# Clustered attention and a routed expert layer on one core: GpSimd's scatters and gathers given fixed places among its low parts, and the first expert's w1 split by way of PSUM

## The chip, the cores and the metric

The kernel runs on one core of one Trainium2 chip. The metric is the device time of one execution in microseconds; lower is better. The engines are named as the profile names them: PE (TensorE, matrix multiplies, with PEld for its weight loads), DVE (VectorE), ACT (ScalarE), POOL (GpSimd) and SP (SyncE, which here only issues DMAs). Each engine takes its own instructions strictly in order. The on-chip memory is SBUF, the accumulators of PE are eight banks of PSUM, and DRAM is the memory outside.

## The reference, cut to what is computed

Attention within clusters (batch 4, 8 heads, 768 positions, head size 64, 16 clusters), whose output rows go through a two-level router to one of 16 experts:

```python
q_assign = argmax(q_n @ c_n.T); k_assign = argmax(k_n @ c_n.T)   # nearest of 16 centroids
mask = q_assign[:, None] == k_assign[None, :]
scores = where(mask, q @ k.T / 8, -1e9)
attn = softmax(scores); x = attn @ v                              # rows: 4*768 tokens of 512
g_idx = argmax(x @ w_group)                                       # 4 groups
e_idx = argmax(x @ w_expert[g_idx])                               # 4 experts in each
h = maximum(x @ w1[g, e], 0.0)                                    # 512 -> 1024
out = g_w * e_w * (h @ w2[g, e])                                  # 1024 -> 512, gates are softmax values
```

Every product is made in 16-bit parts: a float32 number is written as a high part and a low part (what the high part leaves), and the products of the parts are added in PSUM.

## The kernel before, in words

**Attention.** The loop goes over 32 heads (4 batches of 8) and, in each head, over 9 units `u`; a unit is 512 columns of the score matrix. For unit number g, PE makes the fine scores (`fine`, tile `psf`, two banks), ACT takes the exponential into `p` (line 347), and the low part `pl` is made by one subtraction, on GpSimd for all units but some of the last two heads (line 349). That subtraction is called a low part below. Five units later (`LAG = 5`) PE multiplies high and low part with V (`av`, tile `pso`, lines 366 and 367). Eighteen units ahead PE makes the coarse scores of a later head (`coarse`, tile `psc`, two banks), of which DVE takes the row maxima (line 305). The last coarse unit is number 287, so PE makes none from unit 270 on. Beside the units run the splits of q, k and v, the cluster masks and the end of each head (lines 380 to 387), at places given by a table of unit numbers. Work that needs a bank of the small pool `psm` (two banks) takes turns: a generator yields `PSM` and is called when its turn comes, one turn in each unit.

**Router.** After the last head of a batch b, `logits` and `decide` work out each token's expert and its row in a table in DRAM. `decide` then scatters 6 x 128 rows of token number and gate into that table, one indirect DMA of GpSimd for each of 6 columns (line 668), and yields 5 units before each (4 for batch 2). The Tile scheduler, which puts the instructions into each engine's order, is free to move such a DMA ahead in GpSimd's order, since it depends on no low part.

**First expert.** After batch 2 has been decided, `first` picks the expert with most tokens so far, loads its w1 (four chunks of 128 x 1024 float32, tile `st`, four buffers) and splits each chunk: ACT writes the high part `wh` (line 758), and DVE makes the low part `wl` by one instruction with both tensors in SBUF (line 761). Then `first` reads that expert's rows of the table (`tabA`, three DMAs on SP's queue, which wait until all scatters so far have landed), turns them into `idA` (DVE, line 816), gathers 288 token rows with three indirect DMAs of GpSimd (line 889, into the buffers `qx`, `kx` and `vx`), and transposes them on PE (line 899) near the end of attention. `FIRST` is the number of units that it lets pass after each step.

**Experts.** After attention come the first expert, then the 15 others and an overflow block, with weights streamed through `st`; the change does not touch that part.

`issue_after(x)` makes the scheduler put what is made under it behind instruction x; where both are on one engine, this only sets the order there.

Of the kernel before, what the change touches and what calls it, by code (L numbers as in the profile page):

```python
# [13 lines left out]
F32 = mybir.dt.float32  # L14
I32 = mybir.dt.int32
AF = mybir.ActivationFunctionType
ALU = mybir.AluOpType
AX = mybir.AxisListType
ET = mybir.EngineType
# [3 lines left out]
P = 128  # L23
SQ = 16.0
XS = 128.0
WS = 32.0
# [1 line left out]
WRS = 16.0  # L28
PSHIFT = 55.4375
PSM = "psm"  # L30
FIRST = 4

def attention(ctx, tc, qT, kT, vr, cen, R, DEN, cfg):
    nc = tc.nc
# [11 lines left out]
    NH = B * H  # L46
# [288 lines left out]
    def fine(h, u):  # L335
        assert ("max", h) in ready
        pf = ps_f.tile([P, 512], F32, name="psf")
        off = 0
        for (c, q0, q1) in fsegs(u):
            o = pf[:, off:off + q1 - q0]  # L340
            ks = slice(c * P, (c + 1) * P)
            nc.tensor.matmul(out=o, lhsT=KA[h % 8][0:82, ks], rhs=QA[h % 8][0:82, q0:q1], start=True, stop=False)  # L342
            nc.tensor.matmul(out=o, lhsT=KBs[h][:, ks], rhs=QBs[h][:, q0:q1], start=False, stop=True)  # L343
            off += q1 - q0
        p32 = pp.tile([P, 512], F32, name="p32")
        pl = pp.tile([P, 512], F16, name="pl")
        cfg["exp"] = nc.scalar.activation(out=p32, in_=pf, func=AF.Exp, scale=QK / (SQ * SQ))  # L347
        ph = p32.bitcast(BF16)[:, 1::2]
        (nc.vector if u in (EARLY if h < 2 else DVE_LO[h % 8] if h < NH - 2 else DVE_END) else nc.gpsimd).tensor_tensor(out=pl, in0=p32, in1=ph, op=ALU.subtract)  # L349
        Ph[h, u], Pl[h, u] = ph, pl  # L350

    def av(h, u):
# [168 lines left out]
class Router:  # L521
    def __init__(self, ctx, tc, wr, xbuf, table, N, E, BS, cfg):
        nc = self.nc = tc.nc
        self.tc, self.xbuf, self.table, self.N, self.E, self.BS = tc, xbuf, table, N, E, BS
        const = ctx.enter_context(tc.tile_pool(name="rconst", bufs=1))
        self.sm = ctx.enter_context(tc.tile_pool(name="rsm", bufs=1))
        self.ident = cfg["ident"]
        KD = self.KD = wr.shape[1]
        self.const, self.wr = const, wr

# [81 lines left out]
    def decide(self, b, early=None, then=None):  # L612
# [52 lines left out]
        for c in range(T):  # L665
            for _ in range(1 if early else 4 if then else 5):
                yield
            d = self.last["p"] = nc.gpsimd.indirect_dma_start(
                out=self.table, out_offset=bass.IndirectOffsetOnAxis(ap=di[:, c:c + 1], axis=0),
                in_=self.pay[:, t0 + c], in_offset=None)  # L670
            if self.apart:

                self.alone(d, "sent", self.sent)
# [18 lines left out]
class Experts:  # L692
# [61 lines left out]
    def split_chunk(self, st, hi, lo, i, q, eng):  # L754
# [5 lines left out]
            nc.gpsimd.tensor_scalar(out=h, in0=st, scalar1=WS, scalar2=0.0, op0=ALU.mult, op1=ALU.add)  # L760
        nc.vector.scalar_tensor_tensor(out=l, in0=st, scalar=WS, in1=h, op0=ALU.mult, op1=ALU.subtract)

    def wtiles(self, pool, i, n=""):
        w = (self.w1, self.w2)[i]
        sh = [P, w.shape[1] // P, w.shape[2]]
        return [pool.tile(sh, F16, name=f"w{a}{i}{n}") for a in "hl"]
# [4 lines left out]
    def first(self):  # L771

        nc, R, E = self.nc, self.R, self.R.E
        t = self.small("ft", [P, E])
        m = self.small("fm", [P, 1])
        nc.vector.tensor_tensor(out=self.cntA, in0=R.cb, in1=R.ebase, op=ALU.subtract)
        nc.vector.scalar_tensor_tensor(out=t, in0=self.cntA, scalar=float(2 * E), in1=self.io, op0=ALU.mult, op1=ALU.subtract)
        nc.vector.tensor_reduce(out=m, in_=t, axis=AX.X, op=ALU.max)
        nc.vector.tensor_scalar(out=self.oh0, in0=t, scalar1=m, scalar2=None, op0=ALU.is_equal)
        nc.vector.tensor_tensor(out=t, in0=self.oh0, in1=self.io, op=ALU.mult)  # L780
        nc.vector.tensor_reduce(out=self.f0f, in_=t, axis=AX.X, op=ALU.add)
        nc.vector.tensor_copy(out=self.f0i, in_=self.f0f)

        nc.vector.tensor_scalar(out=t, in0=R.cb, scalar1=-1.0, scalar2=float(E * R.BS), op0=ALU.mult, op1=ALU.add)
        nc.vector.tensor_tensor(out=t, in0=t, in1=self.oh0, op=ALU.mult)
        nc.vector.tensor_tensor(out=R.cb, in0=R.cb, in1=t, op=ALU.add)
        yield
        self.f0 = self.load_reg(self.f0i[0:1, 0:1], E - 1)
        self.WA = self.wtiles(self.wa, 0)
        after = lambda: self.tc.issue_after(self.cfg["exp"].ins) if "exp" in self.cfg else ExitStack()  # L790
        chunks = []
        for q in range(4 + 2):
            if q < 4:
                chunks.append(self.load_chunk(0, self.f0, q))
            if q >= 2:
                with after():
                    self.split_chunk(chunks[q - 2], *self.WA, 0, q - 2, 0)
            for _ in range(FIRST):
                yield

        CA, KD = self.CA, R.KD
        nt = -(-CA // P)
        sz = [min(P, CA - t * P) for t in range(nt)]
        tab = self.small("tabA", [P, nt, 2])
        tv = R.table.rearrange("(e s) w -> e s w", s=R.BS)[bass.ds(self.f0, 1)].rearrange("e s w -> (e s) w")
        while R.done < R.B - 2:
            yield
        for t, n in enumerate(sz):
            R.reads(nc.sync.dma_start(out=tab[0:n, t], in_=tv[t * P:t * P + n]))
        self.w2A = [self.load_chunk(1, self.f0, 0)]  # L810
        for _ in range(FIRST):
            yield
        ids = self.small("idA", [P, nt], I32)
        g = self.small("gA", [P, nt])
        for t, n in enumerate(sz):
            nc.vector.tensor_copy(out=ids[0:n, t:t + 1], in_=tab[0:n, t, 0:1])
            nc.vector.tensor_scalar(out=g[0:n, t:t + 1], in0=tab[0:n, t, 1:2], scalar1=1.0 / (XS * WS * WS), scalar2=None, op0=ALU.mult)
        self.colsA = [g[0:n, t:t + 1] for t, n in enumerate(sz)], [ids[0:n, t:t + 1] for t, n in enumerate(sz)]

        rows = R.N - R.N // R.B  # L820
        xgs = []
        for t, n in enumerate(sz):
            self.w2A.append(self.load_chunk(1, self.f0, t + 1))
            xf = self.cfg["ld"].tile([P, KD * P * 3 // 2], F32, name=("qx", "kx", "vx")[t])[:, 0:self.D]
            nc.vector.memset(xf, 0.0)
            xgs.append(xf.bitcast(F16).rearrange("p (a d) -> p a d", a=2))
            if rows:
                self.gather(ids[0:n, t:t + 1], n, xgs[t], rows)
            for _ in range(4):
                yield  # L830
        self.xTA = self.wa.tile([P, 2, KD, CA], F16, name="xTA")
        for t, n in enumerate(sz):
            yield PSM, 2, 2
            with after():
                self.transposed(self.xTA, xgs[t], t, n, R.psm.tile([P, 512], F32, name="psm"))
            yield

# [548 lines left out]
```

## Time and profile before

| What | Value |
|---|---|
| Time, median of 3 runs | 810.94 us (809.08 to 813.51) |
| Profiled execution | 810.6 us, with a span of 808.9 us in the trace |
| Attention in the span | to about 440 us |
| PE busy | 738.6 us (91%) |
| DVE, POOL, ACT busy | 621.1, 497.0, 460.0 us |
| Mean granted clock of PE | 0.963 |

The span is what the trace covers, the time is that of the whole execution, 1.7 us more. PE is the engine with the most work; it is in order, so each of its pauses in attention is a unit that comes later. The share of busy time says little of a single place: what matters is where PE pauses, what released it, and at what clock it went on.

### The profile page before, as it was taken

Reading aid. Unit: us, or ns where it says so; the run is one execution under the profiler, and the core shown is the slowest. Engines: PE = TensorE matmul, PEld = TensorE weight load, DVE = VectorE, ACT = ScalarE, POOL = GpSimd, SP = SyncE. Lnnn points to the kernel's source line nnn. Section 1 sums busy time; section 2 is a strip of 40 time slices with the busy share of each in tenths; the row PEclk is TensorE's granted clock in tenths of the full one; section 3 lists DMA queues with packets and bytes.
Section 4 is the critical chain, followed back from the end, with each engine's and each line's share of the span. In section 5 each row is a group of like instructions: output and inputs, shape, how many; then the busy total and the mean of one; then the engine's idle time right before and its main releaser. Section 6 shows DMA issues by size and latency. Waiting matters only on the chain. (4 is left out here: it accounts for less than half of the span.)

```text
span 808.9 us, 26554 instructions
## 1 busy us (share of the span) xinstructions
PE 738.6 (91%) x11034; PEld 627.1 (78%) x11034; DVE 621.1 (77%) x1193; ACT 460.0 (57%) x893; POOL 497.0 (61%) x497
## 2 busy tenths in 40 slices
PE   5899999989999899997699868999999999999992
PEld 3677788768887688875588655788779999999991
DVE  6998879878798788988865645767589988887840
ACT  4567868658686587765366445435544454555431
POOL 9487787697877878769663424525556544654330
PEclk6899999999999999999799989999999999999996
DMA  8856435235343352223210287866687678888700
GB/s 235 210 155 154 127 100 163 77 90 146 103 138 101 90 144 67 68 74 106 92 41 4 80 296 254 260 215 216 220 262 246 225 246 261 263 274 270 234 30 18
DMA packets 80616, 128.54 MB, mean 159 GB/s; under 512 B 9011, under 2 KB 47411, under 8 KB 80488
## 3 DMA queue, kind: packets, MB, share of 16 engines
q1 hardware_dynamic: 74636, 113.12, 46.8%
q0 software_dynamic: 5696, 13.61, 4.7%
q8 instruction: 88, 1.44, 0.8%
q14 instruction: 40, 0.33, 0.1%
q10 hardware_dynamic: 156, 0.03, 0.0%
HBM read 93.47 MB, written 14.11 MB: 133 GB/s over the span
## 5 line engine op out<-in xcount | busy, mean ns | idle before, releaser
L349 POOL TENSOR_TENSOR pl<-p 128x512 f16<-128x512 f32 x278 | 288.6, 1054 | 98.2 <-ACT p L347 93.8
L305 DVE TENSOR_REDUCE mpart<-psc 128x1 f32<-128x512 f32 (+1 forms) x282 | 190.3, 684 | 47.1 <-PE psc L302 46.6
L347 ACT ACTIVATE p<-psf 128x512 f32<-128x512 f32 x288 | 169.3, 595 | 80.3 <-PE psf L343 72.2
L366 PE MATMUL pso<-V,pl 128*128 128x65 f16 x1152 | 164.0, 195 | 5.5 <-POOL pl L349 5.3
L366 PE MATMUL pso<-V,p 128*128 128x65 f16 x1152 | 164.6, 195 | 0.8 <-issue 0.6
L367 PE MATMUL pso<-V,p 128*128 128x64 f16 x1152 | 163.7, 193 | 0.0
L367 PE MATMUL pso<-V,pl 128*128 128x64 f16 x1152 | 163.7, 192 | 0.0
L342 PE MATMUL psf<-A 82*128 82x384 f16 (+2 forms) x576 | 144.9, 277 | 2.3 <-DMA A<-mr 0.9
L343 PE MATMUL psf<-B 128*128 128x384 f16 (+2 forms) x576 | 145.1, 277 | 0.0
L367 PEld LDWEIGHTS <-p 128*128 128x128 bf16 x1152 | 113.6, 99 | 22.2 <-issue 1.5
L366 PEld LDWEIGHTS <-p 128*128 128x128 bf16 x1152 | 113.2, 98 | 16.8 <-issue 8.9
L302 PE MATMUL psc<-A 80*128 80x512 f16 (+1 forms) x376 | 109.7, 333 | 15.7 <-DVE mpart L305 14.4
L366 PEld LDWEIGHTS <-pl 128*128 128x128 f16 x1152 | 112.3, 97 | 6.5 <-POOL pl L349 5.9
L367 PEld LDWEIGHTS <-pl 128*128 128x128 f16 x1152 | 113.8, 99 | 0.6 <-issue 0.3
L930 DVE SCALAR_TENSOR_TENSOR hl<-psh,hh 128x160 f16<-128x160 f32 (+14 forms) x136 | 50.1, 370 | 56.4 <-ACT hh L929 47.2
L929 ACT ACTIVATE hh<-psh 128x160 f16<-128x160 f32 (+14 forms) x136 | 46.1, 346 | 64.8 <-PE psh L927 63.7
L927 PE MATMUL psh<-xT,wh0a 128*128 128x288 f16 (+7 forms) x512 | 75.6, 256 | 0.9 <-issue 0.5
L988 POOL DMA_INDIRECT out_dram<-y,ri x32 | 38.9, 1215 | 60.3 <-ACT y L987 55.2
L927 PE MATMUL psh<-xT,wh0b 128*128 128x272 f16 (+6 forms) x448 | 65.2, 254 | 1.6 <-ACT xT L901 1.2
L343 PEld LDWEIGHTS <-B 128*128 128x128 f16 x576 | 56.9, 99 | 11.2 <-issue 3.0
L342 PEld LDWEIGHTS <-A 82*128 82x128 f16 x576 | 55.9, 98 | 12.3 <-DMA A<-mr 1.0
L927 PE MATMUL psh<-xT,wl0a 128*128 128x288 f16 (+7 forms) x256 | 64.4, 256 | 1.0 <-issue 1.0
(297 smaller groups left out, 1747.5 us busy)
## 6 DMA issues: line engine op xcount, KB each, us to landing
st<-w SPq DMA_DIRECT2D x128, 512.0 KB
B<-parts SPq DMA_DIRECT2D x64, 192.0 KB
kx<-kT SPq DMA_DIRECT2D x16, 384.0 KB
qx<-qT SPq DMA_DIRECT2D x16, 384.0 KB
vx<-vr SPq DMA_DIRECT2D x16, 384.0 KB
A<-parts SPq DMA_DIRECT2D x32, 192.0 KB
xbuf<-xs SPq DMA_DIRECT2D x4, 1536.0 KB
A<-mk SPq DMA_DIRECT2D x56, 24.0 KB
```

What stands on the lines that cost most here:

```text
L302: last["mm"] = nc.tensor.matmul(out=pc[:, off:off + k1 - k0], lhsT=QA[h % 8][0:80, c * P:(c + 1) * P], rhs=KA[h % 8][0:80, k0:k1], start=T ...
L305: nc.vector.tensor_reduce(out=(mp[:, 0, 0:1], mp[:, :, 1], mp[:, 1, 0:1])[i], in_=pc.rearrange("p (a x) -> p a x", a=n), axis=AX.X, op=ALU ...
L342: nc.tensor.matmul(out=o, lhsT=KA[h % 8][0:82, ks], rhs=QA[h % 8][0:82, q0:q1], start=True, stop=False)
L343: nc.tensor.matmul(out=o, lhsT=KBs[h][:, ks], rhs=QBs[h][:, q0:q1], start=False, stop=True)
L347: cfg["exp"] = nc.scalar.activation(out=p32, in_=pf, func=AF.Exp, scale=QK / (SQ * SQ))
L349: (nc.vector if u in (EARLY if h < 2 else DVE_LO[h % 8] if h < NH - 2 else DVE_END) else nc.gpsimd).tensor_tensor(out=pl, in0=p32, in1=ph, ...
L366: nc.tensor.matmul(out=O[:, col:col + 65], lhsT=p[:, bs], rhs=vh, start=c == 0 and q == 0 and i == 0, stop=False, skip_group_check=True)
L367: nc.tensor.matmul(out=O[:, col:col + 64], lhsT=p[:, bs], rhs=vl, start=False, stop=c == NCH - 1 and i == 1, skip_group_check=True)
L927: self.mm = nc.tensor.matmul(out=ph[:, 0:M], lhsT=w[:, k, fs], rhs=xT[:, a, k], start=i == 0, stop=i == 3 * KD - 1)
L929: nc.scalar.activation(out=hh[:, f], in_=ph[:, 0:M], func=AF.Relu)
L930: self.ev = nc.vector.scalar_tensor_tensor(out=hl[:, f], in0=ph[:, 0:M], scalar=0.0, in1=hh[:, f], op0=ALU.max, op1=ALU.subtract)
L988: d = nc.gpsimd.indirect_dma_start(out=self.out, out_offset=bass.IndirectOffsetOnAxis(ap=idc, axis=0), in_=y[0:n], in_offset=None, bounds_ ...
```

## The change

Three things are changed. The table scatters of batches 0 to 2 and the three gathers of the first expert are each placed behind the latest low part that was given to GpSimd (`cfg["lo"]`). The w1 split of the first expert becomes `split_beside`: the high part as before, and then for each half of a chunk ACT writes the scaled float32 values to a bank of `psm` and DVE subtracts the high part from there; each half takes a turn in the small pool. `FIRST` goes from 4 units to 2 (3 behind the reading of the table).

```diff
-FIRST = 4
+FIRST = 2
...
-        (nc.vector if u in (EARLY if h < 2 else DVE_LO[h % 8] if h < NH - 2 else DVE_END) else nc.gpsimd).tensor_tensor(out=pl, in0=p32, in1=ph, op=ALU.subtract)
+        lo = (nc.vector if u in (EARLY if h < 2 else DVE_LO[h % 8] if h < NH - 2 else DVE_END) else nc.gpsimd).tensor_tensor(out=pl, in0=p32, in1=ph, op=ALU.subtract)
+        if lo.ins.engine == ET.Pool:
+            cfg["lo"] = lo
...
-            d = self.last["p"] = nc.gpsimd.indirect_dma_start(
-                out=self.table, out_offset=bass.IndirectOffsetOnAxis(ap=di[:, c:c + 1], axis=0),
-                in_=self.pay[:, t0 + c], in_offset=None)
+            with self.tc.issue_after(self.cfg["lo"].ins) if self.apart and not early and "lo" in self.cfg else ExitStack():
+                d = self.last["p"] = nc.gpsimd.indirect_dma_start(
+                    out=self.table, out_offset=bass.IndirectOffsetOnAxis(ap=di[:, c:c + 1], axis=0),
+                    in_=self.pay[:, t0 + c], in_offset=None)
...
+    def split_beside(self, st, hi, lo, i, q):
+
+        nc = self.nc
+        h, l = (w[:, *self.part(i, q)] for w in (hi, lo))
+        with self.after():
+            nc.scalar.activation(out=h, in_=st, func=AF.Copy, scale=WS)
+        n = st.shape[1] // 2
+        for j in range(2):
+            yield PSM, 1, 1
+            rows = slice(j * n, j * n + n)
+            t = self.R.psm.tile([P, 512], F32, name="psm").rearrange("p (a b) -> p a b", a=n)
+            with self.after():
+                nc.scalar.activation(out=t, in_=st[:, rows], func=AF.Copy, scale=WS)
+            nc.vector.tensor_tensor(out=l[:, rows], in0=t, in1=h[:, rows], op=ALU.subtract)
...
             if q >= 2:
-                with after():
-                    self.split_chunk(chunks[q - 2], *self.WA, 0, q - 2, 0)
+                yield from self.split_beside(chunks[q - 2], *self.WA, 0, q - 2)
             for _ in range(FIRST):
                 yield
...
         self.w2A = [self.load_chunk(1, self.f0, 0)]
-        for _ in range(FIRST):
+        for _ in range(FIRST + 1):
             yield
...
             if rows:
-                self.gather(ids[0:n, t:t + 1], n, xgs[t], rows)
+                with self.tc.issue_after(self.cfg["lo"].ins) if "lo" in self.cfg else ExitStack():
+                    self.gather(ids[0:n, t:t + 1], n, xgs[t], rows)
```

In the rows below, which list an engine's instructions in order, L is the line of the code, then come the operation and out<-in; a number behind a name tells buffers apart. Line numbers of the changed kernel are up to 21 higher, and 20 lines stand between L816 before and L836 after.

First, GpSimd behind batch 0, where the scatters (`table<-pay,rdi`) go in among the low parts. Before:

```order
L349 TENSOR_TENSOR pl<-p_4053 128x512
L668 DMA table<-pay,rdi 54400x2
L349 TENSOR_TENSOR pl<-p_4082 128x512
L668 DMA table<-pay,rdi 54400x2 x2
L349 TENSOR_TENSOR pl<-p_4116 128x512
L668 DMA table<-pay,rdi 54400x2
L349 TENSOR_TENSOR pl<-p_4145 128x512
L668 DMA table<-pay,rdi 54400x2 x2
L349 TENSOR_TENSOR pl<-p_4173 128x512
```

The same place after:

```order
L349 TENSOR_TENSOR pl<-p_4145 128x512
L349 TENSOR_TENSOR pl<-p_4173 128x512
L672 DMA table<-pay,rdi 54400x2
L349 TENSOR_TENSOR pl<-p_4206 128x512
L349 TENSOR_TENSOR pl<-p_4246 128x512
L349 TENSOR_TENSOR pl<-p_4277 128x512
L349 TENSOR_TENSOR pl<-p_4310 128x512
L349 TENSOR_TENSOR pl<-p_4348 128x512
L672 DMA table<-pay,rdi 54400x2
```

Six scatters among four low parts become one scatter behind every fifth low part; behind batch 1 it is the same, and behind batch 2 there are four low parts between two scatters.

Second, GpSimd at the sixth scatter of batch 2 and the gathers of the first expert (`qx<-xbuf,idA` and so on). Before, the first gather stood nine low parts behind that scatter (`p_9647` is the p of unit 242):

```order
L668 DMA table<-pay,rdi 54400x2
L349 TENSOR_TENSOR pl<-p_9647 128x512
L349 TENSOR_TENSOR pl<-p_9676 128x512
L349 TENSOR_TENSOR pl<-p_9710 128x512
L349 TENSOR_TENSOR pl<-p_9739 128x512
L349 TENSOR_TENSOR pl<-p_9769 128x512
L349 TENSOR_TENSOR pl<-p_9809 128x512
L349 TENSOR_TENSOR pl<-p_9850 128x512
L349 TENSOR_TENSOR pl<-p_9889 128x512
L349 TENSOR_TENSOR pl<-p_9925 128x512
L889 DMA qx<-xbuf,idA 128x1024
```

After (`p_10329` is the p of unit 262, and `p_10470` that of unit 266):

```order
L349 TENSOR_TENSOR pl<-p_10329 128x512
L672 DMA table<-pay,rdi 54400x2
L349 TENSOR_TENSOR pl<-p_10359 128x512
L349 TENSOR_TENSOR pl<-p_10395 128x512
L349 TENSOR_TENSOR pl<-p_10433 128x512
L349 TENSOR_TENSOR pl<-p_10470 128x512
L910 DMA qx<-xbuf,idA 128x1024
L349 TENSOR_TENSOR pl<-p_10524 128x512
L349 TENSOR_TENSOR pl<-p_10560 128x512
L349 TENSOR_TENSOR pl<-p_10591 128x512
L910 DMA kx<-xbuf,idA 128x1024
```

The sixth scatter has moved 21 units back, and the first gather stands four low parts behind it.

Third, DVE around the split of w1 and the reading of the table (`mpart<-psc` are the row maxima of the coarse scores). Before:

```order
L761 SCALAR_TENSOR_TENSOR wl_9582<-st,wh_9581 128x2x512
L387 TENSOR_TENSOR xs<-pso,xs 128x6x64
L305 TENSOR_REDUCE mpart_200<-psc 128x1 x2
L600 COPY lg<-psm 128x60
L305 TENSOR_REDUCE mpart_200<-psc 128x2
L816 CAST idA<-tabA 128x1
```

After, at the end of the split, the last half and what follows it:

```order
L783 TENSOR_TENSOR wl_9582<-psm,wh_9581 128x512
L305 TENSOR_REDUCE mpart_199<-psc 128x2
L305 TENSOR_REDUCE mpart_199<-psc 128x1 x2
L305 TENSOR_REDUCE mpart_199<-psc 128x2
L382 TENSOR_SCALAR DEN<-pso 128x6
L384 RECIPROCAL rec<-DEN 128x6
L387 TENSOR_TENSOR pso<-pso,rec 128x6x64
L305 TENSOR_REDUCE mpart_199<-psc 128x1
L389 TENSOR_TENSOR xs<-pso,xs 128x6x64
L836 CAST idA<-tabA 128x1
```

The four instructions of 1024 columns have become eight of 512, all ahead of `idA`, and `idA` now stands between the sixth and the seventh coarse unit of the last head. On SP's queue the three loads of `tabA` have moved behind two of the loads `A<-mr` (row maxima) and all four loads of the first expert's w2 follow them.

More of the change, by code (lines that the diff above doesn't have):

```diff
@@ L526, in __init__ @@
         self.sm = ctx.enter_context(tc.tile_pool(name="rsm", bufs=1))
-        self.ident = cfg["ident"]
+        self.ident, self.cfg = cfg["ident"], cfg
         KD = self.KD = wr.shape[1]
@@ L761, in split_chunk, with after @@
         nc.vector.scalar_tensor_tensor(out=l, in0=st, scalar=WS, in1=h, op0=ALU.mult, op1=ALU.subtract)
+    def after(self):
+        return self.tc.issue_after(self.cfg["exp"].ins) if "exp" in self.cfg else ExitStack()
+    def split_beside(self, st, hi, lo, i, q):
[11 more added lines that the diff above has]
+            nc.vector.tensor_tensor(out=l[:, rows], in0=t, in1=h[:, rows], op=ALU.subtract)
     def wtiles(self, pool, i, n=""):
@@ L789, in first @@
         self.WA = self.wtiles(self.wa, 0)
-        after = lambda: self.tc.issue_after(self.cfg["exp"].ins) if "exp" in self.cfg else ExitStack()
         chunks = []
@@ L833, in first @@
             yield PSM, 2, 2
-            with after():
+            with self.after():
                 self.transposed(self.xTA, xgs[t], t, n, R.psm.tile([P, 512], F32, name="psm"))
```

## The prediction

> **What bounds the kernel now.** I read the page first: PE's busy slices and its clock.
>
> ```profile
> PE   5899999989999899997699868999999999999992
> PEclk6899999999999999999799989999999999999996
> ```
>
> PE is nearly full from the second slice on. It dips in slices 18 to 19 (364 to 404 us) and a little in 8 and 13, inside attention; the dips at 23 lie behind it, where nothing is moved. So I took PE's busy time by windows around those places (start:end, length, then PE, PEld, DVE, ACT, POOL busy with counts, clock, DMA share, GB/s).
>
> ```profile
> 168.00:175.10 7.10, 3.96 (x67) 3.03 (x65) 4.74 (x9) 3.06 (x6) 6.38 (x8) 0.99 0.57 141
> 175.10:178.30 3.20, 3.18 (x36) 2.37 (x37) 0.62 (x1) 1.24 (x3) 3.20 (x4) 0.50 0.00 0
> 270.00:277.40 7.40, 4.51 (x78) 3.44 (x77) 4.85 (x9) 3.25 (x7) 6.68 (x8) 0.99 0.55 137
> 277.40:280.90 3.50, 3.50 (x60) 2.68 (x58) 1.21 (x2) 1.24 (x3) 3.50 (x4) 0.53 0.02 5
> 380.00:387.20 7.20, 1.71 (x30) 1.37 (x27) 7.20 (x4) 1.80 (x3) 4.58 (x5) 0.72 0.08 7
> 387.20:390.00 2.80, 2.80 (x36) 2.17 (x35) 1.69 (x10) 0.82 (x2) 1.20 (x2) 0.51 0.50 175
> 398.00:402.90 4.90, 0.07 (x2) 0.00 (x0) 4.90 (x4) 0.60 (x1) 3.17 (x4) 0.72 0.00 0
> 402.90:406.60 3.70, 3.69 (x42) 3.01 (x42) 2.72 (x7) 1.29 (x3) 0.61 (x1) 0.50 0.47 146
> 180.00:210.00 30.00, 29.79 (x576) 24.78 (x574) 25.27 (x55) 23.93 (x46) 23.04 (x24) 1.00 0.40 107
> 350.00:360.00 10.00, 10.00 (x198) 8.34 (x195) 8.25 (x20) 6.46 (x13) 7.57 (x8) 1.00 0.06 15
> ```
>
> The last two rows are attention as it runs undisturbed: PE pauses 0.21 us in 30, and a unit takes 1.25 us (24 low parts in 30 us, 8 in 10). The other rows are four stops, each followed by about 3 us at half clock; a busy microsecond at clock 0.50 loses half of itself. A (168): 3.14 idle + 1.6 = 4.7 us. B (270): 2.89 + 1.65 = 4.5. D (380): 5.49 + 1.4 = 6.9. E (398): 4.83 + 1.85 = 6.7. The timeline says what ended them.
>
> ```profile
> 175.12 0.23 PE L366 MATMUL pso<-V,pl 128*128 128x65 f16 x1 [2.17 <-POOL pl L349]
> 277.06 0.20 PE L366 MATMUL pso<-V,pl 128*128 128x65 f16 x1 [2.16 <-POOL pl L349]
> 174.01 8.02 POOL L349 TENSOR_TENSOR pl<-p 128x512 f16<-128x512 f32 x8
> 386.78 0.58 PE L302 MATMUL psc<-A 80*128 80x256 f16 x2 [5.49 <-DVE mpart L305]
> 402.92 0.58 PE L302 MATMUL psc<-A 80*128 80x512 f16 x1 [4.85 <-DVE mpart L305]
> 379.14 6.52 DVE L761 SCALAR_TENSOR_TENSOR wl<-st,wh 128x1024 f16<-128x1024 f32 x1
> 390.76 1.23 DVE L761 SCALAR_TENSOR_TENSOR wl<-st,wh 128x1024 f16<-128x1024 f32 x1
> 396.28 5.97 DVE L761 SCALAR_TENSOR_TENSOR wl<-st,wh 128x1024 f16<-128x1024 f32 x1 [0.72 <-ACT wh L758]
> 375.56 9.02 POOL L349 TENSOR_TENSOR pl<-p 128x512 f16<-128x512 f32 x9
> 397.15 4.03 POOL L349 TENSOR_TENSOR pl<-p 128x512 f16<-128x512 f32 x4
> ```
>
> A and B: PE waits for a low part, and GpSimd is working off eight of them without a pause, because six scatters stood ahead. D and E: PE waits for DVE's maxima, and DVE sits in the w1 subtraction. That instruction takes 1.23 us at 390.76 and 6.52 at 379.14. GpSimd's string of nine low parts ends at 384.58 and the subtraction at 385.66, 1.08 later; the string of four ends at 401.18 and the subtraction at 402.25, 1.07 later. So DVE waited until GpSimd paused. The strings are the backlog of the scatters again.
>
> A fifth stop, C, is smaller: two pauses of PE, behind two tiny instructions of `first` that ended with GpSimd's low part.
>
> ```profile
> 369.35 0.38 PE L302 MATMUL psc<-A 80*128 80x512 f16 x1 [1.43 <-DVE mpart L305]
> 372.85 0.38 PE L302 MATMUL psc<-A 80*128 80x256 f16 x2 [1.05 <-DVE mpart L305]
> 366.94 1.77 DVE L779 TENSOR_SCALAR oh<-ft,fm 128x16 f32<-128x16 f32 x1
> 370.36 0.17 DVE L785 TENSOR_TENSOR ft<-ft,oh 128x16 f32<-128x16 f32 x1
> 370.57 1.63 DVE L786 TENSOR_TENSOR cb<-cb,ft 128x16 f32<-128x16 f32 x1
> 371.11 1.05 POOL L349 TENSOR_TENSOR pl<-p 128x512 f16<-128x512 f32 x1
> ```
>
> C is 1.43 + 1.05 = 2.5 us. All five come to 25.3 us.
>
> The Trainium skill (SBUF — State Buffer, Who interferes with whom) says that a DVE instruction with two SBUF inputs and a GpSimd instruction that reads SBUF exclude each other, and the second waits until the first has finished. The trace agrees on the exclusion but not on the length: 5.4 us, more than five low parts. By the page's one low part, D and E would be short and the split by PSUM worth about 2 us instead of 13; the rows decide.
>
> **The change, part by part.** Prices:
>
> ```profile
> L349 POOL TENSOR_TENSOR pl<-p 128x512 f16<-128x512 f32 x278 | 288.6, 1054 | 98.2 <-ACT p L347 93.8
> L668 POOL DMA_INDIRECT table<-pay,rdi x24 | 25.3, 1053 | 17.8 <-DVE rdi L659 12.4 <-issue 4.8 <-DMA qx<-qT 0.3
> L199 DVE TENSOR_TENSOR parts<-psm,parts 128x384 f16<-128x384 f32 x48 | 26.5, 552 | 2.8 <-ACT psm L198 2.4
> L198 ACT ACTIVATE psm<-qx 128x384 f32<-128x384 f32 x24 | 11.6, 488 | 1.3 <-DVE parts L199 1.3
> ACT psm L198 <- DVE parts L199: 5.0, 11, 0.9
> ```
>
> *Scatters of batches 0 and 1.* A scatter costs GpSimd 1.05 us and 4.8/20 = 0.24 of issue, 1.29. Five low parts and a scatter are 5 x 1.054 + 1.29 = 6.56 us against five units of 6.25: GpSimd falls behind by 0.31 with each, 1.9 with six. Cover: a low part is used five units (6.25 us) after its unit; exponential (0.60) and low part take 1.65 of it, so 4.6 are spare. PE does not stop. Bounds are 0 and 1.9 a batch; I take 0.5, near the undisturbed rows. Gain: 4.7 + 4.5 - 1.0 = 8.2 us.
>
> *The w1 split.* DVE loses four instructions (15.8 us with their waits) and gets eight of 128x512 with one input in PSUM. The nearest row has the same form with 384 columns, at 552 ns on average over 48 while GpSimd makes low parts all the time, so it doesn't wait for pauses; scaled by 4/3 it is 0.74 us, 5.9 in all. ACT gets eight copies, 0.488 x 4/3 = 0.65 each, 5.2 us over some 20 units (25 us); there ACT was busy 6.5 in 10 and DVE 8.3, so both get full but not over. The bank adds waits: the existing copies lost 5.0 us in 48 or 0.10 each, so 0.8 for eight; the worst, 0.9 each, would be 7. I take 1.0. Gain: 6.9 + 6.7 - 1.0 = 12.6 us. The extra turns delay `logits` by a unit or so; its results are due a head later, so nothing.
>
> *C.* The scatters leave this place, the low parts stay. L785 took 0.17 us while a scatter was issued, and the two that waited ended with a low part. After the change all seven small instructions meet low parts only, up to 1.05 us each. Between a gain of 2.5 and a loss as large I take 0.
>
> *The new wait.* `idA` on DVE now comes four units after the sixth scatter, and its data takes this chain:
>
> ```profile
> 459.44 0.96 POOL L668 DMA_INDIRECT table<-pay,rdi  x1 [0.30 <-issue]
> 463.15 0.36 SPq L1055 DMA_DIRECT2D tB<-table  x1
> 465.89 0.15 DVE L1002 CAST bi<-tB 128x1 int32<-128x1 f32 x1 [5.32 <-DMA tB<-table]
> 380.50 1.56 SPq L809 DMA_DIRECT2D tabA<-table  x3
> ```
>
> From the end of batch 3's last scatter (460.40) to SP's next load are 2.75 us, from there to DVE 2.74; the third load of `tabA` starts 1.2 after the first. Let T be the start of unit 262's exponential. With four low parts between scatters GpSimd falls behind by 4 x 1.054 + 1.29 - 5.0 = 0.5 each time, 2.5 by the sixth. That scatter ends at T + 0.60 + 2.5 + 1.05 + 1.29 = T + 5.4, so `idA` is ready at T + 5.4 + 2.75 + 1.2 + 2.74 = T + 12.1. DVE gets there behind the coarse unit made with unit 266, at about T + 6.4, and waits 5.7 us with the next maxima queued behind it. PE has two banks for them: it stops at the third, in unit 269 (T + 8.75), until about T + 12.8. That is 4.0 us, and 1.5 of half clock as behind A. Bounds: 0, if GpSimd is not behind and units run slower, and 8. I take 5.5. GpSimd waits at the first gather too, but less, since that needs the first load only.
>
> The Trainium skill (TensorE: Matmul & The Clock Gate, What's actually happening) lets the clock fall after an idle window of about 3.4 us that runs freely. Here pauses of 2.17 us were enough, with shorter ones ahead. By the page a stop under 3.4 us may keep the clock, and the sum would be 1.5 better; I keep the rows.
>
> *The gathers* come some 25 us later. The third is issued behind the low part of unit 273 and used by PE near unit 286.
>
> ```profile
> 430.03 0.60 ACT L347 ACTIVATE p<-psf 128x512 f32<-128x512 f32 x1 [0.33 <-PE psf L343]
> 466.93 0.99 POOL L889 DMA_INDIRECT xg<-xbuf,bi  x1 [4.39 <-issue]
> 475.28 0.43 DVE L901 COPY xT<-psm 128x512 f16<-128x512 f16 x1 [2.24 <-PE psm L899]
> ```
>
> Thirteen units at 0.93 us are 12; a gather was landed and transposed 8.4 us after its start beside the weight loads. Cost 0, cover about 3.5 us. The w2 loads on SP come behind the `tabA` loads but find their buffers free, ten units before use: 0.
>
> *Sum:* 8.2 + 12.6 + 0 - 5.5 = 15.3 us. The profiled execution took 810.6 (span 808.9 and 1.7 around it), the median of the runs is 810.94, the same within 0.05%. 810.6 - 15.3 = 795.3; I say 795.
>
> **The rivals.**
> 1. *The table wait doesn't show.* For: if ACT's new copies slow the units, DVE comes later to `idA`. Against: 5.7 us is long for that. Then 810.6 - 20.8 = 790, and with C gained 787.
> 2. *The scatters stop PE wherever they stand.* GpSimd has 23 us of work in 30 already, and 6 x 1.29 more fill it; if low parts then come late one by one, A and B come back in small pieces. Against: 4.6 us of cover. Time: 810.6 - 12.6 + 5.5 = 803.5.
> 3. *The split by PSUM waits as before.* If the new subtractions also waited for GpSimd, or ACT's bank waits were the worst, D and E would stay: 810.6 - 8.2 + 5.5 = 808, no measurable change. Against: the L199 row.
> 4. *Slower: the seven small instructions of `first`.* GpSimd's pauses decide here. If GpSimd then runs strings as long as at 375.56, each waits 5.4 us like the subtraction: up to 7 x 5.4 = 38 us of DVE, of which 36 (less two units' cover) would stop PE: 810.6 - 15.3 + 36 = 831. It turns slower than before from 2.6 us each. For: both waiting instructions ended with a low part. Against: the scatters that made the strings now come behind this place. The Trainium skill's rule above (one instruction's wait) would also cap it at about 7 us.
>
> **How the numbers follow.** Forecast 0.62 (790 to 802: the wait between 0 and 8, the bank waits up to 5); rival 1 0.12; rival 2 0.14; rival 3 0.07; rival 4 0.05. Half a percent, 4 us, is what a measurement here can tell from no change. Faster by more: 0.62 + 0.12 + 0.14 = 0.88; same 0.07; slower 0.05. The range goes from 787 (rival 1 with C) to 804 (rival 2) and leaves out about 0.15.
>
> **What the profile after would show.** Right: GpSimd without strings of eight low parts around 170 and 270, PE there as in 180 to 210; eight subtractions near 0.7 us each; PE with one stop near unit 269 released by DVE's maxima, and DVE waiting for the DMA of `tabA` just before it. Wrong: PE waiting for `pl` between spaced scatters (rival 2), the subtractions at over 1.5 us (rival 3), instructions of `first` over 2 us (rival 4), no wait of DVE for `tabA` (rival 1), or a stop of PE for `vx` at the end of attention.

## The result, and the profile after

The changed kernel took 788.87 us (median of 4 runs, 783.38 to 792.52) against 810.91 us of the kernel before, timed beside it: a ratio of 0.972, with a 95% interval of 0.966 to 0.978. The forecast was 795 with a range of 787 to 804. The profiled execution took 788.0 us with a span of 786.3. The same two rows of the page, after:

```profile
PE   5899999999999999998999789999999999999991
PEclk9889999999999999999999999999999999999997
```

Counted from 0, the dips of PE in slices 8, 13, 18 and 19 are gone but for one tenth in slice 18; the dip behind attention is still there. (The clock's 8 in slices 1 and 2 lies before batch 0 is decided; it is a matter of the run, as the repeats show below.)

To see where the time came from, I cut both traces at four marks: the first matmul of `decide` in batches 0, 1 and 2 (from the timelines of before and after) and the first subtraction of the first expert, which I take as the end of attention. Columns: start, length, engine, line, operation, and what ended the idle time ahead.

```profile
158.41 0.20 PE L647 MATMUL psm<-roe,low 128*128 128x96 f16 x1 [1.27 <-DVE roe L635]
260.59 0.20 PE L647 MATMUL psm<-roe,low 128*128 128x96 f16 x1 [1.27 <-DVE roe L635]
362.28 0.20 PE L647 MATMUL psm<-roe,low 128*128 128x96 f16 x1 [1.27 <-DVE roe L635]
444.05 0.45 DVE L930 SCALAR_TENSOR_TENSOR hl<-psh,hh 128x288 f16<-128x288 f32 x1
```

```profile
160.66 0.20 PE L649 MATMUL psm<-roe,low 128*128 128x96 f16 x1 [1.27 <-DVE roe L637]
257.54 0.20 PE L649 MATMUL psm<-roe,low 128*128 128x96 f16 x1 [1.27 <-DVE roe L637]
354.52 0.20 PE L649 MATMUL psm<-roe,low 128*128 128x96 f16 x1 [1.27 <-DVE roe L637]
423.94 0.45 DVE L951 SCALAR_TENSOR_TENSOR hl<-psh,hh 128x288 f16<-128x288 f32 x1
```

The stretch from batch 0's mark to batch 1's (stop A is in it) went from 102.18 to 96.88 us, the next (B) from 101.69 to 96.98, the one from batch 2's mark to the end of attention (C, D, E) from 81.77 to 69.42, and what follows attention from 364.85 to 362.36. The gains are 5.3, 4.7, 12.35 and 2.5; the start lost 2.25. Windows of after (columns as in the prediction) where A was, from there to the next batch, at the one stop that is left, and where `idA` is made:

```profile
163.00:174.00 11.00, 10.81 (x203) 8.79 (x200) 10.01 (x25) 7.30 (x16) 9.13 (x10) 1.00 0.63 155
174.00:254.00 80.00, 79.72 (x1557) 66.80 (x1554) 68.63 (x147) 62.90 (x122) 66.94 (x67) 1.00 0.45 125
366.00:370.00 4.00, 2.64 (x47) 2.09 (x44) 1.77 (x3) 3.10 (x6) 1.96 (x2) 1.00 0.96 348
397.00:401.00 4.00, 3.75 (x83) 3.13 (x81) 2.91 (x11) 2.24 (x6) 3.81 (x5) 1.00 0.89 262
```

PE pauses 0.19 us in 11 and 0.28 in 80: A is gone, and so is B by the length of its stretch. The stop at 366 to 370 was not forecast; the timeline of after shows it, with C's two rests ahead and the chain of the table behind:

```profile
359.65 0.38 PE L302 MATMUL psc<-A 80*128 80x256 f16 x2 [0.73 <-DVE mpart L305]
364.00 0.38 PE L302 MATMUL psc<-A 80*128 80x256 f16 x2 [0.69 <-DVE mpart L305]
366.89 1.06 ACT L775 ACTIVATE wh<-st 128x1024 f16<-128x1024 f32 x1 [1.53 <-DMA st<-w]
369.01 0.27 PE L342 MATMUL psf<-A 82*128 82x256 f16 x1 [1.36 <-ACT p L347]
392.26 0.99 POOL L672 DMA_INDIRECT table<-pay,rdi  x1 [0.16 <-issue]
394.64 1.46 SPq L829 DMA_DIRECT2D tabA<-table  x3
397.39 0.15 DVE L836 CAST idA<-tabA 128x1 int32<-128x1 f32 x1 [0.79 <-DMA tabA<-table]
```

ACT waits for the first chunk of w1, because a chunk is now split four units after its load is issued instead of eight; the next exponential is queued behind it, and PE waits for that. DVE waits 0.79 us for the table ahead of `idA`, where the prediction had 5.7, and PE does not stop behind it (3.75 of 4.00 us busy in the last window). The eight subtractions, as the lines of that source line sum them up (least, median, most ns):

```profile
L783 DVE TENSOR_TENSOR wl<-psm,wh x8: 680/692/693, 368.5 to 389.6; 128x512 f16<-128x512 f32 x8
```

### The profile page after: what moved, and what is told of

It is laid out like the page before. It is cut to its first block, busy times and chain, and to the rows that moved or that the text cites. A ratio compares the mean times of both kernels' runs of the same rounds, so it can differ in the third digit from the quotient of the medians.

```text
span 786.3 us, 26554 instructions
## 1 busy us (share of the span) xinstructions
PE 735.8 (94%) x11034; PEld 625.0 (79%) x11034; DVE 610.6 (78%) x1197; ACT 462.4 (59%) x901; POOL 499.7 (64%) x497
## 5 line engine op out<-in xcount | busy, mean ns | idle before, releaser
L368 PE MATMUL pso<-V,p 128*128 128x65 f16 x1152 | 161.8, 193 | 0.0
L368 PE MATMUL pso<-V,pl 128*128 128x65 f16 x1152 | 161.4, 194 | 0.0
L369 PE MATMUL pso<-V,pl 128*128 128x64 f16 x1152 | 161.2, 191 | 0.0
L369 PE MATMUL pso<-V,p 128*128 128x64 f16 x1152 | 161.0, 191 | 0.0
L1009 POOL DMA_INDIRECT out_dram<-y,ri x32 | 41.6, 1300 | 59.1 <-ACT y L1008 54.1
```

What stands on the lines that cost most here:

```text
L368: nc.tensor.matmul(out=O[:, col:col + 65], lhsT=p[:, bs], rhs=vh, start=c == 0 and q == 0 and i == 0, stop=False, skip_group_check=True)
L369: nc.tensor.matmul(out=O[:, col:col + 64], lhsT=p[:, bs], rhs=vl, start=False, stop=c == NCH - 1 and i == 1, skip_group_check=True)
L1009: d = nc.gpsimd.indirect_dma_start(out=self.out, out_offset=bass.IndirectOffsetOnAxis(ap=idc, axis=0), in_=y[0:n], in_offset=None, bounds_ ...
```

## The experiments

All stretches in one table, from the traces (us; the fourth column is the part behind attention, which no kernel here touches), with the median time and its ratio to the kernel before on the same chip:

| Kernel | b0 to b1 | b1 to b2 | b2 to end of attention | behind | time | ratio (95%) |
|---|---|---|---|---|---|---|
| before | 102.2 | 101.7 | 81.8 | 364.9 | 810.9 | |
| after | 96.9 | 97.0 | 69.4 | 362.4 | 788.9 | 0.972 (0.966-0.978) |
| e1 scatters bound alone | 97.1 | 97.0 | 76.1 | 362.7 | 794.9 | 0.982 (0.979-0.985) |
| e2 split alone | 101.9 | 101.6 | 72.1 | 359.6 | 798.5 | 0.986 (0.982-0.991) |
| e3 split a step later | 97.0 | 97.0 | 67.8 | 360.5 | 785.1 | 0.969 (0.966-0.972) |
| e4 after again | 97.3 | 97.0 | 69.2 | 360.2 | 784.6 | 0.969 (0.966-0.972) |
| e5 halves in SBUF | 96.9 | 97.0 | 74.8 | 366.1 | 791.5 | 0.977 (0.973-0.981) |
| e6 table at once | 97.1 | 97.0 | 70.2 | 364.6 | 790.0 | 0.974 (0.970-0.978) |
| e8 FIRST 4 | 97.3 | 97.0 | 70.2* | 359.2 | 784.9 | 0.969 (0.965-0.972) |
| e9 combination | 97.7 | 98.3 | 68.8* | 362.5 | 789.7 | 0.976 (0.972-0.980) |
| e10 combination, table later | 97.6 | 98.4 | 68.8* | 363.8 | 789.5 | 0.972 (0.970-0.975) |
| e11 first spread | 97.1 | 97.0 | 69.4 | 362.9 | 786.6 | 0.969 (0.966-0.971) |
| e12 after again | 97.3 | 97.0 | 69.5 | 363.1 | 787.3 | 0.971 (0.968-0.973) |

(* Not to be compared with the others: in e9 and e10 batch 2's mark itself stands two units later, and in e8 the first expert starts later among PE's other work, so the second mark has moved.) e1 to e4 ran on one chip in one set, e5 to e9 in a second, e10 to e12 in a third.

**e1 and e2: each part alone.** e1 keeps the bound scatters and gathers and goes back to the old split; e2 keeps the new split and lets the scheduler place scatters and gathers as before.

```diff
 e1
-FIRST = 2
+FIRST = 4
-                yield from self.split_beside(chunks[q - 2], *self.WA, 0, q - 2)
+                with self.after():
+                    self.split_chunk(chunks[q - 2], *self.WA, 0, q - 2, 0)
-        for _ in range(FIRST + 1):
+        for _ in range(FIRST):
 e2, at the scatters (the gathers alike)
-            with self.tc.issue_after(self.cfg["lo"].ins) if self.apart and not early and "lo" in self.cfg else ExitStack():
+            with ExitStack():
```

> The scatters and gathers are bound to their places, the w1 split stays as before (one subtraction a chunk, both inputs in SBUF, FIRST 4). The two cuts must add up if they are independent: before 810.9, after 788.9. Theory 1 (two separate causes): A and B are gone, 10 us; at the split the subtraction still excludes GpSimd, and waits whenever GpSimd is behind. With a scatter every four units GpSimd stays about 1 us behind, so each of the four takes between 2 and 6 us: D and E come back in part, 793 to 801. Theory 2 (only the strings made the subtraction wait, as in the burst of scatters): with the scatters apart GpSimd pauses after nearly every low part, the four take 1.2 to 2.3 us each, and this kernel is as fast as the one with both parts, 788 to 791. Theory 3 (exclusion by itself, strings or not): all four at 5 us and more, 801 to 803.

> The split by way of PSUM with FIRST 2, but the scatters and gathers not bound: they come in bursts as before. A and B must come back: PE waits for a low part at about 175 and 277 by about 2.2 us, and the time rises by 9 to 10 us against the kernel with both parts. Theory 1 (two separate causes): the eight subtractions stay at 0.68 to 0.70 us also beside a string of low parts, since one input is in PSUM; batch 2's burst then makes a stop of PE like A, 4 to 5 us: together 802 to 804. If the burst of batch 2 finds its cover, 798 to 799. Theory 2 (PSUM is not what matters, the strings are): the subtractions beside the string take up to 5 us, DVE is late for the maxima, and the time is 806 to 811.

e1: the stretches of A and B are those of after, to 0.2 us, so these 10 us belong to the scatters' places. So does what C gained: its two waits are 0.73 and 0.69 us here as in after, but 1.42 and 1.04 in e2, where the scatters are not bound. D and E came back smaller. The old subtraction, GpSimd beside it, and PE in the timeline of e1:

```profile
368.83 4.00 DVE L765 SCALAR_TENSOR_TENSOR wl<-st,wh 128x1024 f16<-128x1024 f32 x1
376.93 1.23 DVE L765 SCALAR_TENSOR_TENSOR wl<-st,wh 128x1024 f16<-128x1024 f32 x1 [0.39 <-ACT wh L762]
382.04 5.30 DVE L765 SCALAR_TENSOR_TENSOR wl<-st,wh 128x1024 f16<-128x1024 f32 x1 [0.72 <-ACT wh L762]
368.70 3.03 POOL L349 TENSOR_TENSOR pl<-p 128x512 f16<-128x512 f32 x3
382.22 4.02 POOL L349 TENSOR_TENSOR pl<-p 128x512 f16<-128x512 f32 x4
373.94 0.38 PE L302 MATMUL psc<-A 80*128 80x256 f16 x2 [2.96 <-DVE mpart L305]
387.99 0.59 PE L302 MATMUL psc<-A 80*128 80x512 f16 x1 [4.18 <-DVE mpart L305]
```

GpSimd's strings end at 371.73 and 386.24, the subtractions at 372.83 and 387.34: 1.10 us later both times, as the prediction read it in the kernel before. Even a string of three or four low parts holds DVE to its end. Two of the four subtractions met such a string; the other two took 1.23 and 1.82 us. Theory 1 holds, with 794.9 in its 793 to 801, but not for all four as it had it.

e2: A and B are back, and the split is nearly as good as in after. In its timeline (PE at A and at the split; then GpSimd's longest string, behind three gathers in a burst, and the first and the last of the four subtractions that fall into it):

```profile
175.43 0.24 PE L368 MATMUL pso<-V,pl 128*128 128x65 f16 x1 [2.16 <-POOL pl L349]
378.93 0.27 PE L342 MATMUL psf<-A 82*128 82x256 f16 x1 [2.52 <-ACT p L347]
391.61 13.00 POOL L349 TENSOR_TENSOR pl<-p 128x512 f16<-128x512 f32 x13
392.71 0.69 DVE L783 TENSOR_TENSOR wl<-psm,wh 128x512 f16<-128x512 f32 x1 [0.27 <-ACT psm L782]
400.18 0.68 DVE L783 TENSOR_TENSOR wl<-psm,wh 128x512 f16<-128x512 f32 x1
```

GpSimd works without a pause from 391.61 to 404.61, and each of the four takes 0.68 or 0.69 us in it. So thirteen low parts in a row do not lengthen it; theory 2 is out. The burst of batch 2 made no stop behind `pl`, so the smaller of theory 1's numbers (798 to 799) came true. That the stretch is still 2.7 us longer than in after goes with C, whose waits are back, and with the first chunk of w1, for which ACT waited 2.69 us here and PE behind it 2.52, with a clock of 0.65 after that. The two parts add up: 1.81% (e1) and 1.36% (e2) make 3.17%, and both together gained 3.12% (e4) in the same set.

**e5: PSUM, or only halves?** ACT scales each half in its place in `st`, and DVE subtracts with both inputs in SBUF.

```diff
-            t = self.R.psm.tile([P, 512], F32, name="psm").rearrange("p (a b) -> p a b", a=n)
+            t = st[:, rows]
```

> Both parts, but ACT scales each half in its place in SBUF instead of writing it to a PSUM bank, so that each half's subtraction on DVE has both inputs in SBUF; all else stays. Theory 1 (what counts is that one input is in PSUM): the eight take 0.7 us where GpSimd pauses and wait for its pauses elsewhere, up to 4 to 5 us beside a string of low parts; PE stops again behind DVE's maxima, and the time goes up by 4 to 8 us, about to the kernel with the scatters bound and the old split. Theory 2 (the halves are what counts: DVE gives way sooner): each takes at most 0.7 and one low part, 1.8 us, PE does not stop, and the time is within 2 us of the changed kernel's.

```profile
384.26 3.47 DVE L783 TENSOR_TENSOR wl<-st,wh 128x512 f16<-128x512 f32 x1
383.14 4.03 POOL L349 TENSOR_TENSOR pl<-p 128x512 f16<-128x512 f32 x4
388.85 0.58 PE L302 MATMUL psc<-A 80*128 80x512 f16 x1 [3.14 <-DVE mpart L305]
```

In these rows of e5 a half-sized subtraction takes 3.47 us: GpSimd's string ends at 387.17, the subtraction 0.56 later. The other seven had less to wait for and took 0.68 to 1.57 us. The stretch is 5.4 us longer than in after, within theory 1's 4 to 8, and the time 791.5. So it is the bank of PSUM that counts. There is one stop instead of e1's two, but e5 also has `FIRST` at 2 where e1 has 4, so what the halves give by themselves is not shown. The Trainium skill (SBUF — State Buffer, Who interferes with whom) says that DVE with at most one SBUF input does not contend with GpSimd, outside DVE's two-port modes. The trace agrees: 0.69 us beside a string with one input in SBUF (e2), 3.47 with both (e5).

**e6, e9 and e10: the wait for the table.** The prediction's largest cost hardly showed. e6 takes the rows out that stand between the table's loads and `idA`. e9 starts from e3 and takes out PE's waits for `roe` and C; e10 is e9 with the reading of `idA` put three units later.

```diff
 e6
-        for _ in range(FIRST + 1):
-            yield
 e9, in decide; in first, one more "yield" behind each of four of the small instructions
+        for _ in range(0 if early else 2):
+            yield
         yield PSM, 1, 1
 e10, beside e9's
-        for _ in range(FIRST + 1):
+        for _ in range(FIRST + 4):
```

> Both parts, but idA is read right behind the loads of tabA instead of three units later. It tells whether the chain of the forecast (scatter, load, idA, maxima behind it on DVE, PE) is there and only had its cover. In the changed kernel DVE waited 0.8 us there. Theory 1 (the chain holds, only its lengths were wrong): DVE comes about 3.4 us earlier and waits 4 to 5 us; PE, which has two banks of cover, stops for 2 to 3 us behind the maxima and runs 1 to 1.5 us at half clock: the time goes up by 2.5 to 4.5 us. Theory 2 (such a wait of DVE finds cover): no stop of PE over 0.8 us there, time unchanged within 1 us.

> The split one step later as in the third kernel, and two more pauses taken out of PE's way: the decision of batches 0 to 2 gives two units between the making of roe and its matmuls (PE waited 1.27 us for it each time), and the small instructions of first are spread over four more units (two waits of 0.7 us). Theory 1 (each wait is a mere matter of place): 3 x 1.27 + 1.4 = 5.2 us less than the kernel with the split one step later, if the clock stays full, 779 to 781. Theory 2 (a wait moved is a wait met elsewhere): the scatters, the table and the gathers come six units later, and what is gained is lost at the end of attention: 783 to 786.

> The combination again, but idA is read six units behind the loads of tabA instead of three. In the combination DVE waited 2.08 us for the table, PE stopped for 2.03 us behind it and ran about 3 us at half clock after that. Theory 1 (the table's wait is what the combination lost at the end of attention): that stop goes, 3 to 4 us less than the combination, about as fast as the changed kernel, since two waits of 1.0 us for DVE's maxima took the place of those for roe. Theory 2 (the gathers, three units later, are then late): a stop of PE for a gathered tile at 415 to 425, the time of the combination within 1.5 us.

The timeline of e6, then that of e9 with the window behind its stop:

```profile
397.50 0.15 DVE L834 CAST idA<-tabA 128x1 int32<-128x1 f32 x1 [1.65 <-DMA tabA<-table]
398.37 0.15 DVE L834 CAST idA<-tabA 128x1 int32<-128x1 f32 x1 [0.66 <-DMA tabA<-table]
399.24 0.38 PE L302 MATMUL psc<-A 80*128 80x256 f16 x2 [1.31 <-DVE idA L834]
```

```profile
396.26 0.15 DVE L842 CAST idA<-tabA 128x1 int32<-128x1 f32 x1 [0.57 <-DMA tabA<-table]
398.55 0.15 DVE L842 CAST idA<-tabA 128x1 int32<-128x1 f32 x1 [2.08 <-DMA tabA<-table]
399.79 0.21 ACT L313 ACTIVATE mh<-m 128x6 f16<-128x6 f32 x1 [3.19 <-DVE m L311]
400.54 0.22 PE L342 MATMUL psf<-A 82*128 82x128 f16 x1 [2.03 <-ACT p L347]
165.72 0.38 PE L302 MATMUL psc<-A 80*128 80x512 f16 x1 [1.00 <-DVE mpart L305]
```

```profile
400.60:403.60 3.00, 3.00 (x43) 2.44 (x43) 1.53 (x3) 1.79 (x4) 2.39 (x2) 0.71 0.92 306
```

In e6 DVE came 1.7 us earlier than in after (measured from batch 2's mark), not the 3.4 expected: the scheduler places `idA`, and the pauses of `first` only bound it. It waited 2.3 us in two pieces, and PE 1.31 behind it. So the chain exists (theory 1), at a quarter of the price that I gave it; in the stretch e6 lost 0.7 us against after, less than the 2.5 to 4.5 expected. Its time is 5.1 us above e8's of the same set; in the traced runs the start (batch 0's mark at 161.6 and 156.4) and the part behind attention (364.6 and 359.2) make that difference, and nothing was edited there. Whether it was so in the other runs is not shown. In e9 the second load came late, DVE waited 2.65 us, and the way to PE was another: the heads' maximum `m` behind it on DVE, ACT's `mh`, the exponential queued behind that, and PE stopped 2.03 us and went on at a clock of 0.71. That is the step as forecast, through ACT instead of the banks.

e9 was no gain: 789.7 against the 779 to 781 of its theory 1 and the 783 to 786 of its theory 2. The wait of 1.27 us for `roe` turned into one of 1.00 for DVE's maxima (the row at 165.72), the stretches of batches 0 and 1 grew by 0.7 and 1.3 us, and the table's wait grew. What else in those two stretches costs time, beside waits too short to be listed, stays open. e10 did not try what it should: DVE's order up to `idA` came out the same as in e9, with the same stop of 2.03 us. It is a second measurement of e9 (789.5).

**e3, e8 and e11: the split's places.** e3 splits each chunk one step (two units) later, e8 has `FIRST` at 4, e11 is e3 with the small instructions of `first` spread as in e9.

```diff
 e3
-        for q in range(4 + 2):
+        for q in range(4 + 3):
-            if q >= 2:
-                yield from self.split_beside(chunks[q - 2], *self.WA, 0, q - 2)
+            if q >= 3:
+                yield from self.split_beside(chunks[q - 3], *self.WA, 0, q - 3)
 e8
-FIRST = 2
+FIRST = 4
```

> Both parts, but each chunk is split one step (two units) later after its load. The profile shows ACT waiting 1.53 us for the first chunk, PE 1.36 us behind it, and half a clock for about 2 us. Theory 1: the load is what is late; the wait goes, and the time falls by 1.4 to 2.5 us, to 786.5 to 787.5. Theory 2: the stop only moves, since the split's end, the reading of the table and idA come two units later and something else waits there: 788.5 to 790. A difference under 1.5 us is hardly to be told by the times alone; the window 360 to 380 of the trace (busy time of PE) tells it.

> Both parts, with FIRST at 4 again: two units more between the steps of the w1 split, so that each chunk is split eight units after its load is issued instead of four. Theory 1 (FIRST 2 made ACT wait for the first chunk's load): ACT's wait of 1.5 us and PE's of 1.4 are gone, 1.5 to 2.5 us gained in the stretch from batch 2's decision to the end of attention. Theory 2 (the split that ends later costs as much at the end): the later idA and gathers come into the last heads, PE waits for a gathered tile or DVE's low parts there, and the time is the same or 1 to 3 us more.

> The split one step later, and the small instructions of first spread over four more units; the decisions as in the changed kernel. Theory 1 (C is a crowd of small instructions between DVE's maxima): the two waits of 0.7 us behind batch 2's decision go, 1.4 us less in the stretch from that decision to the end of attention than with the split one step later alone (67.9 us there), and idA, four units later, no longer waits for the table. Theory 2: each small instruction that meets a low part still takes up to 1 us, so one wait of 0.7 us stays, and the stretch keeps its length within 0.7 us. The time, 783 to 786 by both, can hardly tell them apart.

A window of e3, then rows of the timelines of e8 and of e11:

```profile
366.00:370.00 4.00, 4.00 (x73) 3.29 (x71) 1.64 (x3) 3.06 (x7) 3.47 (x4) 1.00 0.95 353
```

```profile
416.18 0.23 PE L590 MATMUL psf<-ident,xs 128*128 128x128 f16 x1 [0.87 <-ACT xs L388]
```

```profile
358.02 0.38 PE L302 MATMUL psc<-A 80*128 80x256 f16 x2 [0.66 <-DVE mpart L305]
361.19 0.38 PE L302 MATMUL psc<-A 80*128 80x512 f16 x1 [0.68 <-DVE mpart L305]
395.95 0.22 PE L590 MATMUL psm<-ident,xs 128*128 128x128 f16 x1 [1.97 <-DVE wl L783]
```

e3: PE does not pause where after lost 1.36 us, and the stretch is 67.8 against 69.2 of e4: theory 1, worth 1.3 us. In the times it cannot be seen (785.1 and 784.6), as was to be expected. e8 removes the same wait, and its attention is ahead of after's: behind batch 2's mark the last product with V ends at 63.8 us instead of 67.1, and batch 3's decision stands at 71.6 instead of 74.5. But the first expert starts later, 1.4 us ahead of that decision instead of 5.1, so that the stretch reads 70.2. That much of theory 2 is there; that it costs anything is not shown. PE's one longer pause at the end is the 0.87 us above, and from batch 2's mark to the end of the trace e8 takes 429.4 us, after, e4 and e12 431.8, 429.4 and 432.6. So what the step from 4 to 2 of `FIRST` was worth by itself stays open. e11: C stays at 0.66 and 0.68, since two of the small instructions still met a low part (0.46 and 0.97 us); and the scheduler put `idA` ahead of the last subtraction: DVE waited 1.41 and 0.66 us for the table, and that subtraction then held PE's transposes for 1.97 us. Theory 2 for C, but the stretch is 1.6 us longer than e3's, more than either theory gave, and my forecast that `idA` would come later was wrong.

**e4 and e12: the changed kernel again.**

> The changed kernel once more, on the same chip as the other three: 787 to 791 expected by every theory, and the same small stops (C, and ACT's wait for the first chunk of w1). The start of its profile (PE's clock between 40 and 156 us) tells whether the dip of clock there, 0.97 against 1.00 before, is the kernel's or the run's: if the run's, it is at 1.00 here and the first 158 us take 2 us less.

> The changed kernel, beside the two others on their chip: 784 to 789, with a wait of DVE for tabA under 1 us and no stop of PE over 0.8 us behind it. The stretch from batch 2's decision to the end of attention takes 69 to 70 us again, and the part behind attention, which the change does not touch, 359 to 365.

784.6 and 787.3 us, with ratios of 0.969 and 0.971 against the first run's 0.972. The stretches repeat to 0.4 us, and so do C, ACT's wait for the first chunk (PE 1.26 and 1.38 us) and a wait for the table that now stopped PE for 0.59 and 0.58. What differs between runs lies elsewhere: batch 0's mark stands between 156.4 and 161.6 us in the thirteen traces, and the part behind attention takes 359.2 to 366.1, in no relation to the edits. The clock's dip in after's slices 1 and 2 is in e4's slices 0 and 1 instead. So the 2.5 us behind attention and the 2.25 lost at the start are the run's, not the change's. No kernel here beats the changed one by more than such runs of the same kernel differ.

## Why the prediction was right, and which terms were off

- **A and B** were forecast at 8.2 and measured at 10.0 (5.3 + 4.7). The stops were sized nearly right (9.2), and places alone remove them (e1). The half microsecond kept back for each was not needed: GpSimd falls behind by less than 4.6 us of cover.
- **The w1 split**, 12.6. The subtraction's price was right (0.74 forecast, 0.69 measured, from a row of another width), and so was the reason, that one input in PSUM doesn't wait (e2, e5). D and E are gone. But the bank waits of 1.0 were the wrong thing to charge: the one pause of PE over 0.4 us between C and the end of attention came from the load of the first chunk, 1.36 us, which the step "the w1 split" never looked at. `FIRST` went from 4 to 2, and the prediction did not ask how long before its use the load is then issued.
- **C**, 0 forecast, 1.06 gained (2.48 to 1.42 us of pauses). The prediction left the choice between gain and loss open; the gain came with the scatters' places (1.42 and 1.04 us in e2, 0.73 and 0.69 in e1). The longest of the small instructions takes 0.98 us in after, within the one low part that the prediction allowed each; rival 4's strings did not come.
- **The new wait**, 5.5 us forecast, is the step that failed. In after it stopped PE by nothing, in e4 and e12 by 0.6. All three pieces of the chain were too long. GpSimd's lag by the sixth scatter was about 1.0 instead of 2.5, because I priced a low part at the mean length of a row, 1.054 us, while back to back the rows overlap and a new one starts every 1.00 (the row with x8 in 8.02 stood in the prediction), and a scatter at 1.29 where 1.15 came. From the scatter's end (393.25) to SP's load 1.39 us passed instead of 2.75, taken from a single row at another place. And the last load's data was there at most 2.92 us after the first load's issue, instead of 1.2 + 2.74. With T at 389.47 in after, `idA`'s data was there at T + 8.1 instead of T + 12.1, and DVE came at T + 6.9. Between bounds of 0 and 8 I had chosen in the upper half. The mechanism is real, as e6 and e9 show; its size was not. This was rival 1's outcome (790, or 787 with C), though for another reason than the one given there. The one stop of PE near unit 269, by which the forecast was to be known, is in no run of the changed kernel at the size forecast; the time lies in the range because the range reached down to rival 1.
- **The gathers** cost nothing, as forecast.
- One reading was wrong without touching the sum: the row of four low parts at 397.15 is cut off by the window it was asked for. GpSimd's string there is seven long, from 394.15 to 401.17, so E's subtraction, begun at 396.28, waited through five of them; its end, on which the argument rests, was read rightly.

By stretches: A and B 1.8 more than forecast, the rest of attention 12.35 instead of 12.6 - 5.5 = 7.1, so 5.2 more; these 7.0 would have made it 788.3.

## What to carry to other kernels

An elementwise pass of DVE with both inputs in SBUF beside a GpSimd that works in strings should be given one input in PSUM, if a bank and ACT have room; and DMAs that GpSimd issues should be bound one by one among its other work, or they make the strings. Price a chain of waits by the row of the thing itself, undisturbed, and not by a group's mean; where a pause depends on which of two arrivals is later, work out both and keep the difference, not the sum of pessimistic ends. When a stage's distance is shortened, look up when each of its inputs was asked for.

## What the runs showed of the hardware

- A pause of PE of about 2 us is not always followed by a slower clock. These windows are those right behind a pause: of 2.16 and of 2.52 us (e2), of 2.96 and of 4.18 (e1), and of 3.14 (e5).

```profile
175.50:178.50 3.00, 3.00 (x34) 2.18 (x35) 0.51 (x1) 1.13 (x3) 3.00 (x4) 0.50 0.00 1
379.20:382.20 3.00, 3.00 (x37) 2.34 (x36) 2.60 (x6) 2.47 (x6) 2.79 (x3) 0.65 0.31 99
```

```profile
374.00:377.00 3.00, 3.00 (x64) 2.47 (x64) 2.28 (x7) 1.65 (x4) 1.83 (x2) 1.00 0.10 9
388.00:391.00 3.00, 3.00 (x32) 2.32 (x32) 2.02 (x6) 0.61 (x2) 0.19 (x1) 0.50 0.03 6
```

```profile
389.00:392.00 3.00, 3.00 (x34) 2.14 (x33) 2.49 (x5) 0.96 (x3) 1.73 (x3) 0.50 0.01 0
```

  The clock was 0.50, 0.65, 1.00, 0.50 and 0.50: the pause of 2.96 us cost no clock, the one of 2.16 did. Length alone does not decide; where a pause falls does, as far as these traces show. In all thirteen traces each stretch at half clock lasts 3.41 us or a multiple of it, and in the kernel before two of them begin 61 steps of 3.413 us apart (174.89 and 383.10). I cut each trace into pieces on that grid. Between batch 0's mark and the end of attention, each of the eleven pieces at full clock in which PE paused for 1.81 us or more was followed by half clock, and none in which it paused for 1.53 or less. The 2.96 us of e1 lie across a cut (first two rows: 3.42 - 1.89 and 3.41 - 1.98), the 2.16 of e2 almost wholly in one piece, with shorter pauses beside it (last row: 3.41 - 1.33 = 2.08):

```profile
369.09:372.51 3.42, 1.89 (x31) 1.49 (x30) 3.42 (x1) 2.40 (x5) 3.21 (x4) 1.00 0.08 23
372.51:375.92 3.41, 1.98 (x44) 1.70 (x44) 3.11 (x7) 0.57 (x2) 2.20 (x2) 1.00 0.01 0
171.89:175.30 3.41, 1.33 (x21) 0.95 (x21) 2.03 (x5) 1.00 (x2) 2.92 (x3) 1.00 0.19 45
```

  So about half of a piece idle was enough. Ahead of batch 0's mark and behind attention the two do not part so cleanly (1.26 to 1.97 us occur with either outcome), and that is open. The Trainium skill (TensorE: Matmul & The Clock Gate, What's actually happening) has a window of about 3.4 us that runs freely. The grid agrees with that; that it takes at least one idle window, as the skill has it, the trace does not bear out if the whole window is meant.
- DVE with both inputs in SBUF did not start when GpSimd's current low part ended; where the next low part was ready it waited for the first pause, through three and four low parts (e1), three (e5), and the last six and five of their strings (D and E in the kernel before). Its work then ended 1.07 to 1.10 us behind the string for 1024 columns and 0.56 for 512.
- A scatter cost GpSimd 0.96 to 0.99 us in most rows, and 1.78 where it met the old subtraction (e1, at 386.41); SP's next load came 1.39 us behind the last one in after, and 2.75 behind batch 3's in the kernel before.
